# A WKV recurrence and a squared-ReLU feed-forward on one core: another hand-written order of the same instructions

## The chip, the cores and the metric

The kernel runs on one core of one Trainium2 chip. The metric is the device time of one execution in microseconds (us), the median of the runs. A core has a matrix engine (TensorE, PE in the profile; its weight loads are listed as PEld), three engines for elementwise work (VectorE is DVE, ScalarE is ACT, GpSimd is POOL), and SyncE (SP), which here only issues DMAs.

## The reference

The first stage is a recurrence over 768 steps for 4 batches and 8 heads of width 48, with a decay `w` for each step and channel; the second is a feed-forward layer on the 3072 rows that it gives:

```python
for t in range(S):                     # r, k, v, w: (4, 8, 768, 48), u: (8, 48)
    cur = np.einsum('bhd,bhe->bhde', u[None] * kt, vt)
    y[:, :, t] = np.einsum('bhd,bhde->bhe', rt, state + cur)
    state = wt[:, :, :, None] * state + np.einsum('bhd,bhe->bhde', kt, vt)
...
x = attn_out.transpose(0, 2, 1, 3).reshape(B * S, H * D)      # (3072, 384)
h = x @ w_in                                                  # w_in: (384, 2048)
g = np.maximum(h, 0.0) ** 2
return g @ w_out                                              # w_out: (2048, 384), output float32
```

## The kernel before

The 3072 rows are cut into 12 steps of 256 rows, three for each batch (steps 0 to 2 are batch 0). Within a step, two rows share a partition (index `j`), and the 128 partitions are two chunks of 64 (index `c`). The state is carried from chunk to chunk and from step to step of a batch.

What runs on which engine and in which order is written out by hand: `ORDER` is one long string of words, and the program calls one small function for each word from left to right. On each engine the instructions run in the order in which their words stand; between engines only semaphores order them. A word is `name.step...`; `=A`, `=V` or `=G` names the engine (ACT, DVE, POOL), and `:0` to `:3` or `:n`, `:m` a PSUM bank. There are two wide accumulators `att` (banks 0 and 1 for `cum_`, `su_`, `y_` and `p_`) and four narrow ones `one` (banks 0 to 3 for `m1_`, `m2_`, `pw_`, `tr_`, `yt_`; `p_ ... :n` uses 0 and 1 of them).

One step s runs through these words (line of the profile in brackets):

- `ld.s.w`, `.r`, `.k`, `.v`: loads of 384 KB each, issued by SP (L212). `ld.g.i` and `ld.g.o` load quarter g of the input and output weights, 768 KB each (L220, L225); `cast.i.g` and `cast.o.g` round them to 16 bits (L232). `ld.0.u` is a row that `ub_` and `uc_` spread over the partitions.
- `ww_` (L297) multiplies the two rows' decays, `lw_` (L301) takes the logarithm, `cum_` (L341 to L345) sums it over the rows by matmuls, `exp_` and `ac_` (L358, L363) take exponents. `ni_` (L353) replaces one of the matmuls in steps 8 to 11.
- `rw_` and `kw_` (L309, L313) multiply r and k by a decay, `rd_.s.0` and `rd_.s.1` (L376) multiply r and k by the summed decays. Step 0 does this in halves, `rd_.0.i.f`.
- `tr_` (L385) transposes the two on PE in steps 0 to 2, and `rkt_` (L390) copies them out of PSUM; from step 3 on `dtr_` (L393) transposes them by DMA.
- `p_` (L410) multiplies the transposed pair, `pm_` (L418, L421) masks the product. `su_` (L433) forms the new part of the state, `ts_` (L441, L443) adds the old one, `sn_` (L447) applies the decay. `v_` (L305) rounds v.
- `ku_`, `qp_`, `q_`, `vq_` (L316, L321, L324, L327) form the term of the step's own row with u.
- `y_`, `yq_`, `yc_`, `yb_`, `yd_` (L460) add up the stage's output, `ysb_` (L510, L512) copies it out; `yt_` and `xt_` (L520, L525) transpose it on PE in steps 0 to 3, `dyt_` (L528) by DMA from step 4 on.
- `m1_.s.0` to `.7` (L538): the first product of the feed-forward, six matmuls each; `rl_` (L545 on ACT, L547 on DVE) the ReLU, `sq_` (L553, L555) the square. Words 0 and 1 need weight quarter 0, words 2 and 3 quarter 1, and so on.
- The second product: `m2_.s.c.q` (L561, four matmuls, output quarter q) and `os_` (L567, L569) in steps 0 to 4. Steps 5 to 11 use a scheme with seven half-size products, `pw_.s.1` to `.7` (L615), with sums of blocks formed by `tw_` (L580) and `sw_` (L593), and `cx_` and `ow_` (L620 to L634) for the results. `store` (L639) writes them.
- `warm_.n.i` (L643) is n matmuls on zeros whose result nobody reads.

Of the kernel before, what the change touches and what calls it, by code (L numbers as in the profile page):

```python
# [27 lines left out]
rw_.2=G rl_.0.6=A ld.3.o ku_.2=G rl_.1.0=A m1_.1.2:3 m1_.1.4:1 sq_.0.0=A rd_.2.0 tr_.2.1:0 m1_.1.6:2 rl_.1.2=V
rl_.1.4=A m1_.1.1:1 rl_.1.6=V qp_.2=G m1_.1.7:3 rkt_.2.1=V tr_.2.0:2 rl_.1.7=V v_.2=G m1_.1.3:0 rkt_.2.0=V cast.o.0=A
m1_.1.5:3 ac_.2 cast.o.1=G ld.3.k sq_.0.2=A sq_.0.1=A rl_.1.1=V m2_.0.1.0:2 rl_.1.3=A q_.2 sq_.1.0=A p_.2.1:0 su_.2:1  # L30
vq_.2=G sq_.1.1=A m2_.0.1.1 m2_.0.0.0:0 m2_.1.0.0:1 ts_.2.0=V ld.3.r sn_.2.0=G pm_.2.1 m2_.1.0.1 ww_.3=G yc_.2:1
sq_.0.3=A rl_.1.5=A cast.o.2=A yq_.2 p_.2.0:0 sq_.1.2=V m2_.0.0.1 m2_.1.1.0:3 pm_.2.0 lw_.3 sq_.1.3=A m2_.0.0.2
ww_.4=G cum_.3:0 ld.3.v ld.4.r ld.4.k exp_.3 kw_.3=G cast.o.3=A yb_.2 y_.2 m2_.1.1.1 ku_.3=V m2_.1.1.2 m2_.0.1.2
rd_.3.1 rw_.3=G ysb_.2=A lw_.4 m2_.0.1.3 m2_.1.1.3 dtr_.3.1 qp_.3=G rd_.3.0 cum_.4:1 ac_.3 exp_.4 os_.0.1=A os_.1.1=V
m2_.1.0.2 yt_.2:3 tw_.3=V m2_.0.0.3 xt_.2=A rw_.4=G q_.3 m2_.1.0.3 dtr_.3.0 os_.0.0=A kw_.4=G ku_.4=G m1_.2.2:3 ac_.4
os_.1.0=A rd_.4.0 m1_.2.0:0 rl_.2.2=A m1_.2.3:2 ld.4.v v_.3=A rd_.4.1 m1_.2.1:3 rl_.2.0=A su_.3:1 ld.5.w rl_.2.3=A
ld.5.k ld.5.r vq_.3=V p_.3.0:0 rl_.2.1=A ld.7.w m1_.2.6:1 m1_.2.4:2 ts_.3.0=V pm_.3.0 sq_.2.0=A sn_.3.0=G m1_.2.7:3
v_.4=G rl_.2.6=A ts_.3.1=V tw_.1=V yc_.3:1 yq_.3 sq_.2.1=A rl_.2.4=A rl_.2.7=A p_.3.1:0 m2_.2.1.0:0 m1_.2.5:1 ld.5.v
pm_.3.1 rl_.2.5=V ww_.5=G lw_.5 sq_.2.3=A qp_.4=V q_.4 sn_.3.1=G rw_.5=G kw_.5=G y_.3 store.0.1 yb_.3 su_.4:0 dtr_.4.0
m2_.2.0.0:2 ts_.4.0=V ww_.7=G ysb_.3=A m2_.2.0.1 sq_.2.2=A yt_.3:3 cum_.5:1 m2_.2.1.1 m2_.2.0.2 m2_.2.1.2 exp_.5  # L40
sn_.4.0=V store.1.1 rd_.5.1 dtr_.4.1 xt_.3=A m2_.2.1.3 ts_.4.1=V rd_.5.0 v_.5=G vq_.4=G ld.6.w os_.2.1=A m1_.3.4:1
m1_.3.2:3 m1_.3.0:0 ld.6.k rl_.3.4=A ac_.5 rl_.3.2=A rl_.3.0=A dtr_.5.1 sn_.4.1=V ku_.5=V qp_.5=V tw_.2=V m2_.2.0.3
su_.5:1 p_.4.1:0 m1_.3.5:3 ts_.5.0=V os_.2.0=A rl_.3.5=A m1_.3.1:0 pm_.4.1 m1_.3.3:2 dtr_.5.0 rl_.3.1=A m1_.3.7:3
sq_.3.0=A kw_.6=G rl_.3.3=V yc_.4:1 yq_.4 p_.4.0:0 m2_.3.1.0:1 pm_.4.0 sq_.3.2=A sq_.3.1=A rl_.3.7=A m1_.3.6:2 ld.6.r
ld.7.k ld.8.k ww_.6=G sn_.5.0=G ku_.6=G y_.4 yb_.4 ysb_.4=A q_.5 p_.5.0:0 pm_.5.0 store.2.1 m2_.3.1.1 m2_.3.0.0:0
vq_.5=G lw_.6 dyt_.4 tw_.4=V cum_.6:1 p_.5.1:0 rw_.6=G pm_.5.1 rl_.3.6=A exp_.6 m2_.3.0.1 m2_.3.0.2 m2_.3.1.2 ld.7.r
rd_.6.1 ku_.7=G lw_.7 sq_.3.3=A ld.6.v yc_.5:0 yq_.5 y_.5 m2_.3.1.3 dtr_.6.1 os_.3.1=A qp_.6=V rd_.6.0 kw_.7=G
m1_.4.3:2 m2_.3.0.3 rw_.7=G ac_.6 m1_.4.1:1 rl_.4.3=V yb_.5 rl_.4.1=A store.2.0 ysb_.5=V cum_.7:1 q_.6 v_.6=G qp_.7=G
m1_.4.2:3 dtr_.6.0 ac_.7 exp_.7 dyt_.5 m1_.4.0:2 rl_.4.2=A m1_.4.7:1 rl_.4.0=A m1_.4.5:3 vq_.6=G rd_.7.1 os_.3.0=A
rd_.7.0 m1_.4.6:2 rl_.4.7=A ld.7.v m1_.4.4:1 q_.7 sq_.4.0=V rl_.4.5=A rl_.4.6=A ld.8.r ld.8.w su_.6:0 p_.6.0:1  # L50
ts_.6.0=V sq_.4.3=A rl_.4.4=A m1_.5.6:0 pm_.6.0 sn_.6.0=G m1_.5.4:3 ts_.6.1=V m1_.5.7:2 rl_.5.7=A rl_.5.4=A v_.7=G
ku_.8=V p_.6.1:1 yq_.6:0 yc_.6 m1_.5.0:1 m1_.5.5:2 pm_.6.1 rl_.5.6=V rl_.5.0=A m2_.4.0.0:3 sq_.4.2=A sq_.4.1=A
m1_.5.2:1 qp_.8=G sn_.6.1=G rl_.5.5=A y_.6 ww_.8=G su_.7:1 yb_.6 q_.8 dtr_.7.1 dtr_.7.0 ld.9.w m2_.4.0.1 m2_.4.1.0:0
m2_.4.0.2 ts_.7.0=V rw_.8=V rl_.5.2=A vq_.7=V sn_.7.0=V ld.8.v store.1.0 ysb_.6=A lw_.8 sq_.5.3=A cum_.8:0 dyt_.6
ts_.7.1=V kw_.8=V ac_.8 sq_.5.2=A m2_.4.1.1 p_.7.0:1 m2_.4.0.3 ni_.8=V sn_.7.1=G exp_.8 m1_.5.1:2 m1_.5.3:1 m2_.4.1.2
sw_.5.1.1=G store.0.0 pm_.7.0 ld.9.k rl_.5.3=A ld.10.w ld.9.r ww_.9=G vq_.8=G rd_.8.1 m2_.4.1.3 sw_.5.1.2=V rl_.5.1=A
os_.4.0=A rd_.8.0 m1_.6.6:1 os_.4.1=V sq_.5.0=V yc_.7:1 yq_.7 p_.7.1:0 kw_.9=G dtr_.8.0 pm_.7.1 m1_.6.5:2 m1_.6.7:3
m1_.6.4:0 v_.8=A rl_.6.6=A y_.7 lw_.9 sq_.5.1=A sw_.5.0.1=V rl_.6.5=A sw_.5.0.2=V ku_.9=V sw_.5.0.3=V su_.8:0
ts_.8.0=V rl_.6.4=A store.3.0 yb_.7 ysb_.7=A m1_.6.1:2 rl_.6.1=A dtr_.8.1 m1_.6.3:1 sn_.8.0=G rw_.9=V pw_.5.1:0 dyt_.7
sq_.6.2=A rl_.6.3=V cum_.9:1 cx_.5.1=V pw_.5.2:2 ni_.9=V ww_.10=V rl_.6.7=A m1_.6.0:1 ld.9.v exp_.9 ld.10.k ow_.5.1=V  # L60
m1_.6.2:3 sq_.6.3=A rl_.6.0=V rd_.9.1 pw_.5.5 sw_.5.0.4=G sw_.5.1.4=G p_.8.0:0 ac_.9 cx_.5.3=A pm_.8.0 pw_.5.6
m1_.7.2:1 qp_.9=G rd_.9.0 pw_.5.3 rl_.6.2=A rl_.7.2=A sq_.6.0=A yc_.8:0 yq_.8 ld.11.w dtr_.9.1 p_.8.1:1 ku_.10=G
# [638 lines left out]
```

## Time and profile before

| | us |
|---|---|
| median of 3 runs | 177.27 (177.14 to 177.4) |
| the profiled execution, its own time | 178.94 |
| its span, first to last instruction | 177.2 |
| PE busy | 167.7 |
| PE weight loads busy | 132.9 |
| DVE busy | 148.6 |
| ACT busy | 128.6 |
| POOL busy | 113.1 |

The times of single instructions below are from the profiled execution, from the start of its span. Matmuls are pipelined, so a row's duration for one matmul is longer than the distance to the next; the distances between starts tell what PE needs. The granted clock of PE is 1.0 throughout.

### The profile page before, as it was taken

The page shows a single profiled execution, that of the slowest core. Times are in us where ns is not written, and L with a number is a line of the kernel's source. Part 1 is how long each engine was busy: PE and PEld are TensorE (multiplying, and loading weights), DVE is VectorE, ACT ScalarE, POOL GpSimd, SP SyncE. Part 2 cuts the span into 40 slices and gives each one's busy share as a digit, 9 for nine tenths or more (in the row PEclk, how much of TensorE's full clock was granted, in tenths as well). Part 3 has the DMA queues.
Part 4 walks back from the last instruction along what each step waited for, and adds up shares of the span by engine and source line. Part 5 has one row for each costly group of instructions (what it writes and reads, how often), then busy time and mean ns, then how long its engine had stood idle before and what let it go on. Part 6 is the DMA issues. An engine that isn't in the chain of part 4 may idle for free.

```text
span 177.2 us, 6475 instructions
## 1 busy us (share of the span) xinstructions
PE 167.7 (95%) x2772; PEld 132.9 (75%) x2774; DVE 148.6 (84%) x235; ACT 128.6 (73%) x213; POOL 113.1 (64%) x108
## 2 busy tenths in 40 slices
...
GB/s 151 315 311 350 367 266 357 230 369 286 218 257 233 237 256 191 304 253 101 286 199 306 233 156 286 172 238 236 134 257 67 51 45 41 140 89 4 89 10 167
DMA packets 82669, 36.58 MB, mean 206 GB/s; under 512 B 75857, under 2 KB 81106, under 8 KB 82642
## 3 DMA queue, kind: packets, MB, share of 16 engines
...
## 4 chain that ended last, share of the span: by engine, by line
PE 76%; DMA 13%; POOL 4%; DVE 2%; SPq 1%; issue 1%; ACT 0%; DVEq 0%
PE one L538 29%; PE one L615 18%; PE one L561 15%; PE att L460 6%; DMA rkT_b<-rdec_buf 6%; DMA w_st_b<-in_moe_w_out_dram 5%; PE att L410 3%; DMA u_row<-in_u_dram 2%; PE att L433 2%; SPq L212 1%; POOL ku_b L316 1%; PE att L343 1%; POOL wo_sb L232 1%; DVE pmT_b L418 1%; POOL k_b L313 1%
## 5 line engine op out<-in xcount | busy, mean ns | idle before, releaser
L538 PE MATMUL one<-xT_b,wi_sb 128*128 128x256 bf16 x576 | 70.9, 273 | 0.5 <-DVE xT_b L525 0.5
L538 PEld LDWEIGHTS <-wi_sb 128*128 128x128 f16 x576 | 54.7, 98 | 9.1 <-issue 1.2
L545 ACT ACTIVATE gt_b<-one 128x512 f16<-128x512 f32 x73 | 42.1, 598 | 16.2 <-PE one L538 14.8
L553 ACT ACTIVATE gt_b<-gt_b 128x1024 bf16<-128x1024 f16 x39 | 40.1, 1052 | 0.1
L561 PE MATMUL one<-wo_sb,gt_b 128*128 128x384 f16 x160 | 29.5, 326 | 0.4 <-POOL wo_sb L232 0.4
L421 DVE TENSOR_TENSOR pmT_b<-att,mask 128x1024 bf16<-128x1024 f32 x22 | 26.8, 1218 | 1.9 <-PE att L410 1.8
L615 PEld LDWEIGHTS <-gt_b 128*128 128x128 bf16 x280 | 23.5, 98 | 0.6 <-issue 0.2
L561 PEld LDWEIGHTS <-gt_b 128*128 128x128 bf16 x160 | 14.8, 98 | 9.5 <-issue 0.6
L547 DVE TENSOR_SCALAR gt_b<-one 128x512 f16<-128x512 f32 x23 | 15.5, 684 | 3.2 <-ACT gt_b L545 1.9
L447 POOL TENSOR_TENSOR S_b<-t_b,ac_buf 128x192 bf16<-128x192 f32 x16 | 8.8, 551 | 13.8 <-DVE t_b L443 7.7
L327 POOL TENSOR_TENSOR vq_b<-v_b,q_b 128x768 bf16<-128x768 f32 x10 | 15.5, 1550 | 2.7 <-DVE q_b L324 2.7
L615 PE MATMUL one<-wo_sb,gt_b 128*128 128x192 f16 x168 | 16.5, 246 | 0.0
L316 POOL TENSOR_TENSOR ku_b<-k_b,u_bc 128x768 f32<-128x768 f32 x8 | 14.5, 1815 | 2.9 <-ACT u_bc L249 1.8
L313 POOL TENSOR_TENSOR k_b<-k_b,w_b 128x384 f32<-128x384 f32 x10 | 11.0, 1099 | 7.1 <-DMA k_b<-in_k_dram 7.1
L321 POOL TENSOR_TENSOR ku_b<-ku_b,r_b 128x768 f32<-128x768 f32 x8 | 14.9, 1858 | 0.5 <-DVE pmT_b L421 0.4
L309 POOL TENSOR_TENSOR r_b<-r_b,w_b 128x384 f32<-128x384 f32 x9 | 10.7, 1185 | 5.0 <-DMA r_b<-in_r_dram 4.8
L324 DVE TENSOR_REDUCE q_b<-ku_b 128x16 f32<-128x768 f32 x12 | 11.4, 946 | 1.7 <-POOL ku_b L321 1.7
L376 DVE TENSOR_TENSOR rdec_buf<-k_b,att 128x768 bf16<-128x768 f32 (+1 forms) x13 | 11.4, 885 | 1.0 <-POOL k_b L313 0.9
L376 DVE TENSOR_TENSOR rdec_buf<-r_b,att 128x768 bf16<-128x768 f32 (+1 forms) x13 | 11.5, 885 | 0.3 <-POOL r_b L309 0.3
L358 ACT ACTIVATE att<-att 128x768 f32<-128x768 f32 x12 | 9.6, 797 | 2.7 <-PE att L345 2.3
L615 PE MATMUL one<-w_st_b,gt_b 128*128 128x192 f16 x112 | 11.4, 246 | 0.0
L593 POOL TENSOR_TENSOR w_st_b<-w_st_b,gt_b 128x512 bf16<-128x512 bf16 x4 | 5.0, 1250 | 7.5 <-DVE w_st_b L593 7.5
...
## 6 DMA issues: line engine op xcount, KB each, us to landing
...
rkT_b<-rdec_buf SPq DMA_TRANSPOSE x18, 4.4
```

What stands on the lines that cost most here:

```text
L313: product("kw_", s)(k_raw[:, :, 0, :], k_raw[:, :, 1, :], w_raw[:, :, 1, :])
L316: product("ku_", s)(buf("ku", s)[:], buf("k", s)[:, :, 1:3, :], u_bc[:, :, None, :].to_broadcast([C, H, 2, D]))
L321: product("qp_", s)(ku[:], ku[:], buf("r", s)[:, :, 0:2, :])
L327: product("vq_", s)(buf("vq", s)[:].rearrange("p j h d -> p h j d"), buf("v", s)[:], buf("q", s)[:, :, :, None].to_broadcast([C, H, 2, D]))
L376: nc.vector.tensor_mul(rdec[:, i, :, heads, 0:D], x.rearrange("p h j d -> p j h d"), decay[:, None, :, :].to_broadcast([C, 2, n, D]))
L421: nc.vector.tensor_mul(pmT, ps_p[:].rearrange("p e (a x) -> p (e a) x", a=2), mk.to_broadcast([C, 4, 2 * C]))
L538: nc.tensor.matmul(ps1[:, j, :], wi_sb[:, n // 4, kk, n % 4 * 128:(n % 4 + 1) * 128], xT[:, :, kk, :], start=(kk == 0), stop=(kk == KT - 1))
L545: nc.scalar.activation(rl, m1, AF.Relu, scale=RS)
L547: nc.vector.tensor_scalar(out=rl, in0=m1, scalar1=RS, scalar2=0.0, op0=ALU.mult, op1=ALU.max)
L553: nc.scalar.activation(gt, rl, AF.Square)
L561: nc.tensor.matmul(m2, gt[:, n, c * C:(c + 1) * C], wo_sb[:, n, :], start=(n == 0), stop=(n == NT - 1))
L615: nc.tensor.matmul(where_to, gt[:, n, :], wo[:, n, :], start=(n == 0 and i in (1, 2, 5)), stop=(n == NT // 2 - 1), skip_group_check=True)
```

## The change

Only the string `ORDER` is replaced. Both strings have 934 words, and apart from `warm_` the same ones. They differ in the place of the words, in the engine of some (`=`), and in banks (`:`). The idle matmuls of the opening are cut otherwise: 2, 9, 1, 1, 1, 9 before and 1, 3, 6, 5, 3, 12 after. Net changes of engines: seven `rl_` from ACT to DVE, four `rkt_`, three `ysb_` and three `ts_` from DVE to ACT, two `sq_` from DVE to ACT, three `os_` from ACT to DVE, four weight casts off ACT (three to POOL, one to DVE), three `ku_` from POOL to DVE and three `qp_` from DVE to POOL. The opening up to the first `m1_`, and the places of step 2 and step 10 that the text speaks of:

```diff
-ld.0.w ld.0.r warm_.2.3 ld.0.k ld.0.u ww_.0=V lw_.0 ld.0.v warm_.9.0 rw_.0=G ld.1.w ld.1.r cum_.0:1 kw_.0=V exp_.0
-ub_:0 ld.1.k rd_.0.0.1 warm_.1.2 warm_.1.2 rd_.0.1.1 uc_=A ku_.0=G tr_.0.0.1:1 ld.1.v rd_.0.1.0 rkt_.0.0.1=A
-tr_.0.1.1:3 warm_.1.2 rkt_.0.1.1=A tr_.0.1.0:0 ww_.1=G rd_.0.0.0 ld.0.i v_.0=A rkt_.0.1.0=V tr_.0.0.0:2 ld.2.i
-p_.0.1:0 ac_.0 rkt_.0.0.0=V su_.0:1 qp_.0=G pm_.0.1 ld.1.i lw_.1 ts_.0.0=A p_.0.0:n ld.3.i ld.2.w cum_.1:0 kw_.1=G
-pm_.0.0 warm_.9.3 ac_.1 exp_.1 q_.0 ld.2.k rw_.1=G v_.1=A rd_.1.1 sn_.0.0=G vq_.0=G rd_.1.0 tr_.1.1:3 yc_.0:0 yd_.0
-cast.i.0=A ld.2.r rkt_.1.1=V tr_.1.0:2 y_.0 rkt_.1.0=V yq_.0 ts_.0.1=V p_.1.1:n ku_.1=G ysb_.0.1=A p_.1.0:1 sn_.0.1=G
-pm_.1.1 ysb_.0.0=A yt_.0.1:2 cast.i.2=A su_.1:0 yt_.0.0:3 xt_.0.1=V xt_.0.0=V qp_.1=V m1_.0.0:2 ts_.1.0=V cast.i.1=A
...
+ld.0.w ld.0.r ld.0.k warm_.1.1 warm_.3.3 ld.0.u warm_.6.1 ld.1.w ww_.0=V ld.0.v lw_.0 cum_.0:1 warm_.5.0 exp_.0
+kw_.0=V rw_.0=V ld.1.v ub_:0 rd_.0.0.1 uc_=A rd_.0.0.0 ld.1.r tr_.0.0.1:3 ld.1.k ww_.1=G rkt_.0.0.1=A rd_.0.1.1
+tr_.0.0.0:0 rd_.0.1.0 rkt_.0.0.0=A tr_.0.1.1:2 ld.0.i v_.0=G rkt_.0.1.1=A warm_.3.1 ld.2.i ld.2.w ku_.0=V tr_.0.1.0:1
+p_.0.1:0 rkt_.0.1.0=A ac_.0 pm_.0.1 qp_.0=G p_.0.0:n lw_.1 su_.0:1 ld.1.i ts_.0.0=A pm_.0.0 ld.3.i cum_.1:0 warm_.12.2
+q_.0 ld.2.r kw_.1=G ac_.1 exp_.1 rw_.1=G rd_.1.1 sn_.0.0=G v_.1=A cast.i.0=A rd_.1.0 vq_.0=G tr_.1.1:3 yd_.0:0 ku_.1=G
+ld.2.k tr_.1.0:0 rkt_.1.0=V ts_.0.1=V qp_.1=G rkt_.1.1=A yq_.0 yc_.0 y_.0 sn_.0.1=V p_.1.1:n ysb_.0.1=A su_.1:1
+ysb_.0.0=A yt_.0.1:2 pm_.1.1 xt_.0.1=A yt_.0.0:3 p_.1.0:0 xt_.0.0=A cast.i.2=A ts_.1.0=V m1_.0.0:3 ww_.2=G ld.2.v
+pm_.1.0 sn_.1.0=V m1_.0.1:0 m1_.0.5:2 cast.i.1=G q_.1 rl_.0.5=A m1_.0.4:1 rl_.0.4=A lw_.2 vq_.1=V ts_.1.1=V rl_.0.1=A
+y_.1:0 m1_.0.3:2 yc_.1 yq_.1 rl_.0.0=V cast.i.3=G yd_.1 ld.0.o ysb_.1=A ld.1.o cum_.2:1 m1_.0.2:1 exp_.2 rw_.2=G
...
+rkt_.2.0=A q_.2 ld.3.r m1_.1.0:0 rl_.1.4=A m1_.1.5:2 ld.3.o p_.2.1:0 ww_.3=V rl_.0.6=V p_.2.0:1 m2_.0.0.0:1 cast.o.1=G
+rl_.1.0=A sq_.1.0=A lw_.3 rl_.1.5=A sq_.1.1=A sq_.1.3=A ld.4.w vq_.2=G sn_.2.0=G m2_.0.0.1 pm_.2.1 m2_.0.1.0:0
...
+cx_.6.2=A pw_.6.5 v_.10=A cx_.6.3=A pw_.6.7 exp_.11 rl_.8.7=A m1_.8.6:3 rd_.10.0 qp_.10=G rw_.11=G ow_.6.4=V rd_.10.1
+pw_.6.3 rl_.8.6=A kw_.11=V pw_.6.4 dtr_.10.0 m1_.8.0:2 pw_.7.1:3 v_.11=A dtr_.10.1 store.5.1 q_.10 ow_.6.2=V ac_.11
+ow_.6.3=A vq_.10=G rd_.11.0 ac_.10 rl_.8.0=A rd_.11.1 sq_.8.3=A cx_.7.1=V m1_.9.1:1 m1_.9.4:0 rl_.9.1=A pw_.7.2:2
+ow_.7.1=V sw_.7.1.2=G p_.10.0:0 su_.10:1 dtr_.11.0 dtr_.11.1 m1_.9.6:1 ts_.10.0=V pm_.10.0 sn_.10.0=G pw_.7.5 pw_.7.6
...
```

130 lines of the change are left out of this document (61 added, 69 removed).

## The prediction

> **What bounds the kernel now.** I read the page's busy times first, then stretches of the span, then the waits, and then the opening in order of time, since the change is an order and only shows where an engine stands idle. The page and three stretches (columns: us; busy us and count of PE, PE weight loads, DVE, ACT, POOL; clock, DMA share, GB/s):
>
> ```profile
> span 177.2 us, 6475 instructions
> ...
> PE 167.7 (95%) x2772; PEld 132.9 (75%) x2774; DVE 148.6 (84%) x235; ACT 128.6 (73%) x213; POOL 113.1 (64%) x108
> ```
> ```profile
> 10.00:15.00 5.00, 3.38 (x66) 1.82 (x67) 4.62 (x7) 2.86 (x7) 5.00 (x6) 1.00 1.05 325
> 15.00:20.00 5.00, 3.98 (x147) 3.02 (x144) 4.11 (x9) 3.50 (x4) 3.84 (x4) 1.00 1.01 355
> ...
> 120.00:130.00 10.00, 10.00 (x124) 9.22 (x119) 9.31 (x19) 8.85 (x16) 5.22 (x4) 1.00 0.80 190
> ```
>
> TensorE (PE) is full from about 20 us on at the full granted clock; its holes lie before that, where the DMA engines are full (share 1.01 to 1.05). The waits of PE say how little is left after the opening (us in total, times, longest):
>
> ```profile
> PE one L538 <- DVE xT_b L525: 0.5, 1, 0.5
> ...
> PE one L561 <- POOL wo_sb L232: 0.4, 1, 0.4
> PE att L410 <- DMA rkT_b<-rdec_buf: 0.4, 1, 0.4
> PE one L615 <- DVE w_st_b L634: 0.4, 1, 0.4
> ```
>
> The list changes no product except idle `warm_` matmuls: the same matmuls stand in both orders. So the time is the sum of PE's own stream, which stays, the empty time before the first `m1_` (here at 20.00), the few waits after it, and the tail. The opening in order of time (start, duration, what; in brackets the idle time before it and what ended it):
>
> ```profile
> 12.74 1.00 POOL L313 TENSOR_TENSOR k_b<-k_b,w_b 128x384 f32<-128x384 f32 x1
> ...
> 13.69 1.00 POOL L309 TENSOR_TENSOR r_b<-r_b,w_b 128x384 f32<-128x384 f32 x1
> ...
> 14.73 0.95 DVE L376 TENSOR_TENSOR rdec_buf<-r_b,att 128x768 bf16<-128x768 f32 x1
> ...
> 15.12 1.48 POOL L327 TENSOR_TENSOR vq_b<-v_b,q_b 128x768 bf16<-128x768 f32 x1
> 15.60 0.68 DVE L390 COPY rkT_b<-one 128x1024 bf16<-128x1024 bf16 x1
> ...
> 15.83 0.51 PE L460 MATMUL att<-S_b,rkT_b 64*64 64x48 bf16 x24 [0.43 <-DVE rdec_buf L376]
> ...
> 16.50 1.47 ACT L232 CAST wi_sb<-w_st_b 128x1536 f16<-128x1536 f32 x1 [2.37 <-DMA w_st_b<-in_moe_w_in_dram]
> ...
> 17.68 0.42 PE L410 MATMUL one<-rkT_b 64*64 64x128 bf16 x16
> ...
> 17.88 0.85 ACT L512 CAST y_sb_b<-att 128x384 bf16<-128x384 f32 x2
> ...
> 18.13 1.29 DVE L418 TENSOR_TENSOR pmT_b<-one,mask 128x512 bf16<-128x512 f32 x2 [0.24 <-PE one L410]
> ...
> 19.33 0.61 DVE L525 COPY xT_b<-one 128x384 bf16<-128x384 bf16 x2
> ...
> 20.00 3.61 PE L538 MATMUL one<-xT_b,wi_sb 128*128 128x256 bf16 x30 [0.50 <-DVE xT_b L525]
> ...
> 20.77 1.47 ACT L232 CAST wi_sb<-w_st_b 128x1536 f16<-128x1536 f32 x1 [0.66 <-DMA w_st_b<-in_moe_w_in_dram]
> ```
>
> To be seen: `kw_.1` (12.74), `rw_.1` (13.69), `rd_.1.0` (14.73) and then PE at 15.83 form one chain; the first cast of the input weights waits for its landing at 16.5; the copies `rkt_.1.*` are on DVE and run beside that cast; the last link is `xt_.0.*` on DVE, behind `pm_.1.1`.
>
> **The opening, step by step.** Two things that the title names stand in both lists: `ld.0.r` is second and `ld.0.i` is ahead of every load of step 2. What moves on SP's queue is `ld.1.w` ahead of `ld.0.v`, `ld.1.v` ahead of `ld.1.r` and `ld.1.k`, and `ld.2.w` ahead of `ld.1.i` and `ld.3.i`. All loads pass through one queue of full DMA engines, so a load that changes places takes the landing of the place. The two tiles' issues and landings over the first 20 us:
>
> ```profile
> L212 SPq DMA_DIRECT2D k_b<-in_k_dram x3: 1059/1529/5577, 1.9 to 13.7; - x3
> ...
> DMA to landing us min/median/max: 4.8/5.2/11.6
> ```
> ```profile
> L212 SPq DMA_DIRECT2D v_b<-in_v_dram x2: 389/769/1149, 4.2 to 8.2; - x2
> ...
> DMA to landing us min/median/max: 4.1/4.6/5.1
> ```
>
> The second load of v was issued at 8.2 and took 5.1: 13.3. That place is now k of step 1's. So `kw_.1` on POOL starts at 13.4 and not at 12.74, `rw_.1` ends at 15.4, and `rd_.1.0` runs 15.4 to 16.35 where it ended at 15.68: 0.67 later. POOL is emptier before that (`rw_.0` and `ku_.0` go to DVE, `v_.0` comes), but it now waits for the landing, so this gives nothing. On DVE `rw_.0` and `ku_.0` come ahead of `pm_.0.1`, `pm_.0.0` and `q_.0`; these end by about 14.3, still ahead of the 14.4 at which `kw_.1` lets `rd_.1.1` go, so they cost nothing; if k of step 1 landed earlier they would be late next, by up to the 0.6. PE waits with `yd_.0` for `rd_.1.0`, as it did with `yc_.0`, to 16.5.
>
> The larger step is on ACT: `rkt_.1.1` moves from DVE to ACT and behind `cast.i.0` in its order. That cast waits for the same bytes as before, so it runs 16.5 to 17.97 again, though `tr_.1.1` is done by 16.1. What the copy costs on ACT follows from two copies of other sizes:
>
> ```profile
> L525 ACT COPY xT_b<-one 128x768 bf16<-128x768 bf16 x2 | 1.6, 806 | 0.0
> ...
> L390 ACT COPY rkT_b<-one 128x512 bf16<-128x512 bf16 x2 | 1.1, 588 | 0.3 <-PE one L385 0.3
> ```
>
> 512 elements take 588 ns, 768 take 806, so 1024 take 1.02 us: `rkt_.1.1` ends at 19.0, and `p_.1.1` starts at 19.05 instead of 17.68. Behind it on ACT are the two `ysb_.0` (0.85: to 19.85) and the two `xt_.0` (estimated like them, 0.85: to 20.75). `xt_.0` no longer waits for `pm_.1.1`, which gives part of the delay back. `m1_.0.0` starts at 20.8: **0.8 later**. From below: if ACT is free of the cast by then, what is late next is `vq_.0` (1.48 after `sn_.0.0` behind `rw_.1`, to 17.35), then `yq_.0`, `yc_.0`, `y_.0`, the copies and transposes, and `m1_.0.0` at 20.3, 0.3 later. I take 0.8, because the 16.50 is a landing and nothing ahead of it in the queue gets shorter.
>
> The quarters `i.1` and `i.3` land one load later, 384 KB at 325 GB/s, 1.2 us: 22.0 for the first (20.77 above). It is cast on POOL to 23.5; PE arrives at `m1_.0.3` after four `m1_` and `y_.1`, at 24.0. Nothing, then; without that cover up to 0.5. The warm matmuls stand where PE is idle anyway (12 before `tr_.1.1`, done at about 15.2, and it starts at 15.45).
>
> **A rule against the change.** Products that move to DVE beside a busy POOL may not run beside it. The trace has such a pair (the third row is the mean of DVE's four `ku_`):
>
> ```profile
> 42.00 1.00 POOL L313 TENSOR_TENSOR k_b<-k_b,w_b 128x384 f32<-128x384 f32 x1 [2.40 <-DMA k_b<-in_k_dram]
> 42.03 1.79 DVE L316 TENSOR_TENSOR ku_b<-k_b,u_bc 128x768 f32<-128x768 f32 x1 [1.97 <-DMA k_b<-in_k_dram]
> ```
> ```profile
> L316 DVE TENSOR_TENSOR ku_b<-k_b,u_bc 128x768 f32<-128x768 f32 x4 | 4.6, 1159 | 2.0 <-DMA k_b<-in_k_dram 2.0
> ```
>
> The other three took (4.6 - 1.79)/3 = 0.95, so this one lost about 0.84. The Trainium skill, page "SBUF — State Buffer", section "SBUF: two separate sides", says that a DVE instruction with two SBUF inputs and a GpSimd instruction share a port pair under an exclusive lock, and that the later one blocks fully. By that rule, and the trace agrees here with 1.79 against 0.95, `ku_.0` would wait for `v_.0` and the sum would be 177.8 and not 177.7. From the rows alone: `ku_.0` takes between 0.95 and 1.79, the landing of k covers most of it, and 0 to 0.1 reaches `rd_.1.1`; I take 0.
>
> **After the opening.** The second quarter of the output weights is cast at 33.87, which PE awaited:
>
> ```profile
> 33.87 1.47 POOL L232 CAST wo_sb<-w_st_b 128x1536 f16<-128x1536 f32 x1 [1.23 <-DMA w_st_b<-in_moe_w_out_dram]
> ...
> 35.38 2.76 PE L561 MATMUL one<-wo_sb,gt_b 128*128 128x384 f16 x16 [0.42 <-POOL wo_sb L232]
> ...
> 38.39 0.39 PE L410 MATMUL att<-rkT_b 64*64 64x128 bf16 x16
> ```
>
> `ld.1.o` has the same bytes ahead of it in both lists, so the cast ends at 35.35 again. PE would come 0.8 later and finds it done: the wait of 0.42 goes. `p_.2.0` (0.39) moves ahead of that matmul, so the wait stays gone with a smaller delay too. Net here: 0.8 - 0.42 = **0.4 later**.
>
> In the middle, two waits of 0.4 remain in the list above. For the matrix transposes by DMA (rows of 120 to 140 us, and two pieces of the chain that price PE's words):
>
> ```profile
> DMA to landing us min/median/max: 3.0/4.2/4.4
> ```
> ```profile
> 126.82 1.31 PE one L538 x12
> 128.13 3.30 PE one L615 x40
> ```
>
> One `m1_` or `pw_` is 0.655. Step 9's last transpose gets 5.3 us of PE work ahead of its user where it had 3.7, so its 0.4 goes. Step 10's last `rd_` has seven such words, 4.6 us, ahead of `p_.10.0`, where it had 8.7; it needs 0.95 + 3.0 to 4.4: a wait of 0 to 0.8. The other 0.4 (before a `pw_`, on DVE) may go or come. Over the whole, ACT gives away, net, 7 `rl_` (598 ns, the row below), four weight casts (1.47) and three `os_`, and takes four `rkt_`, three `ysb_` and two `sq_`: about -3 us. POOL takes three of the casts and three `qp_` for three `ku_`: about +3. DVE comes out at about +1.5. They are idle for 29 to 64 us of the span, so none becomes the bound over the whole.
>
> ```profile
> L545 ACT ACTIVATE gt_b<-one 128x512 f16<-128x512 f32 x73 | 42.1, 598 | 16.2 <-PE one L538 14.8
> ```
>
> I put the middle at 0, between -0.8 and +1.2. The tail has the same last `pw_`, `ow_.11.3` and one store in both lists: 0.
>
> The sum, made on the profiled run (178.94 us with its span of 177.2, that is 1.7 above the median of the three runs, so I carry differences): 0.8 - 0.42 + 0, **0.4 later; 177.27 + 0.4 = 177.7 us**.
>
> **Rivals.** *Faster:* the opening is set by landings, not by ACT. If the first weight quarter is cast before `tr_.1.1` is done, `m1_.0.0` slips by 0.3 only, the wait of 0.42 at 35.38 hides it, and the waits at step 9's transposes and before the `pw_` go: 0.3 - 0.42 - 0.8, 176.4 us. It decides from a landing before about 15.5; the 16.50 speaks against it, the lighter POOL for it. *Same:* the slip is 0.8 but one of the two middle waits goes and nothing comes: 177.3. *Much slower:* the short distance of step 10 and the DMA transposes of steps 4 and 5, which also get less PE work behind them, each make PE wait 0.5: 0.4 + 1.3, 179.0. For it: the waits of the middle are on just such transfers; against it: the queue ahead of them is shorter. *No change of what the title names:* true for the two loads as said, it has no price of its own.
>
> **Chances.** A run of this kernel can be told from another by about 0.2%, 0.35 us. The forecast (0.3 to 0.9 later) 0.40, much slower 0.17, same 0.18, faster 0.25. The edge of the forecast's case lies within 0.35 for a small part, so: faster 0.25, within 0.2% 0.20, slower 0.55. The range runs from 176.4, the faster case whole, to 179.2, the much slower case and 0.2 for a first cast later than 16.5; what lies outside, waits on several transposes at once or none at all, I give 0.2.
>
> **What would show it.** In the changed profile: `kw_.1` on POOL idle until k's landing at about 13.3; an ACT copy of 128x1024 into `rkT_b` at about 18.0, right behind the cast at 16.5, about 1.0 long; the first `m1_` at 20.3 to 20.8; no wait of PE on `wo_sb` at 35; PE full after it with waits of about 1 us in sum. A first `m1_` at 20.0 or earlier, or a PE wait of over 1 us on a transpose, would make it wrong.

## The result, and the profile after

The changed kernel took **179.66 us** (median of four runs, 178.87 to 181.06) against 177.34 for the kernel before (four runs, 177.14 to 177.46): a ratio of 1.0128, 95% interval 1.0089 to 1.0167, **1.3% slower**, 2.3 us. The forecast was 177.7 us, 0.4 us slower. A second set (e9 below) gave 1.0137 (1.0091 to 1.0184). Some executions of most kernels were in a slower state of the chip and are left out of the ratios; the profiles of e11, e14 and e17 caught one, so no size is read from them.

Below, "after" is the changed kernel, and e1 to e18 are the experiments. A number such as 1.0137 (1.0091 to 1.0184) is the ratio to runs of the kernel before on the same chip, with its 95% interval.

The page of the profiled execution (its own time 180.04 us):

```profile
span 178.3 us, 6502 instructions
PE 169.9 (95%) x2781; PEld 133.4 (75%) x2781; DVE 145.9 (82%) x234; ACT 127.1 (71%) x212; POOL 115.8 (65%) x110
q8 instruction: 22, 0.36, 0.8%
```

The opening in order of time (start, duration, engine, what; in brackets the idle time before it and what ended it), from the timeline:

```profile
9.62 0.82 POOL L305 CAST v_bf_b<-v_b 128x768 bf16<-128x768 f32 x1 [0.19 <-DMA v_b<-in_v_dram]
...
9.71 1.54 DVE L316 TENSOR_TENSOR ku_b<-k_b,u_bc 128x768 f32<-128x768 f32 x1
...
14.01 1.00 POOL L313 TENSOR_TENSOR k_b<-k_b,w_b 128x384 f32<-128x384 f32 x1 [0.86 <-DMA k_b<-in_k_dram]
...
16.14 1.47 ACT L232 CAST wi_sb<-w_st_b 128x1536 f16<-128x1536 f32 x1 [1.33 <-DMA w_st_b<-in_moe_w_in_dram]
...
17.52 1.00 ACT L390 COPY rkT_b<-one 128x1024 bf16<-128x1024 bf16 x1
...
18.97 0.86 ACT L512 CAST y_sb_b<-att 128x384 bf16<-128x384 f32 x2 [0.45 <-ACT rkT_b L390]
...
19.89 0.86 ACT L525 COPY xT_b<-one 128x384 bf16<-128x384 bf16 x2
...
20.80 0.38 PE L538 MATMUL one<-xT_b,wi_sb 128*128 128x256 bf16 x2 [0.22 <-ACT xT_b L525]
```

This is the chain of the prediction, link by link: `kw_.1` (14.01) waits for k, `rkt_.1.1` (17.52) stands behind the cast, and the first `m1_` starts at 20.80. The waits of PE behind the opening (us in total, times, longest), first after, then in a profile of the kernel before with eight idle matmuls at its very end instead of one (e2 below). The first line of e2's list is the wait ahead of the first `m1_` itself:

```profile
PE one L538 <- DMA xT_b<-y_sb_b: 0.5, 1, 0.5
PE one L538 <- ACT xT_b L525: 0.2, 1, 0.2
PE att L410 <- DMA rkT_b<-rdec_buf: 0.2, 1, 0.2
```
```profile
PE one L538 <- DVE xT_b L525: 0.6, 1, 0.6
PE one L615 <- DVE w_st_b L634: 0.4, 1, 0.4
```

To be seen: after, a matrix transpose by DMA (`dyt_`, into `xT_b`) holds PE. In e2, which has the order of before, none does, and there is no wait on `wo_sb` or on `rkT_b` either: the 0.42 and the 0.4 that the prediction read were of the one execution shown. Last, the tail: SP's issue of `store.11.0`, the last store but one, after and before.

```profile
173.30 1.59 SPq L639 DMA_DIRECT2D out_dram<-w_st_b  x1
```
```profile
173.54 0.33 SPq L639 DMA_DIRECT2D out_dram<-w_st_b  x1
```

The DMA view of after for 172 to 175 us shows what moved at that time: the stores on q1, and one packet on q8.

```profile
q1 hardware_dynamic: 276, 0.28, 27.6%
q8 instruction: 1, 0.02, 3.3%
```

It is the 22nd fetch of program code on that queue, 16 KB, 172.96 to 174.52; before there were 21, the last at 162.91. The two stores issued just ahead of the slow one were late too: they landed 3.6 and 3.5 us behind their issue, where the same two took 1.6 and 1.9 in a second profile of after (e9). The first explanation to test was therefore this fetch: after has seven more idle matmuls, 14 more instructions on PE, and PE's program, if this queue serves it, passes one 16 KB step more.

A table cuts every profile into three parts: the start of the first `m1_`, the **stretch** from there to the start of the last matmul of the last `pw_`, and the **tail** from there to the end of the span (us, from the traces):

| kernel | first `m1_` | stretch | tail | span |
|---|---|---|---|---|
| before, as shown to the prediction | 20.00 | 153.46 | 3.70 | 177.2 |
| before, 8 idle at the end (e2) | 20.07 | 151.55 | 3.70 | 175.3 |
| before, 4 idle at the end (e3) | 20.79 | 151.85 | 3.70 | 176.3 |
| before, 16 small idle (e5) | 19.94 | 151.77 | 4.06 | 175.8 |
| before, after's opening parts (e8) | 21.15 | 151.58 | 3.69 | 176.4 |
| after | 20.80 | 152.49 | 4.97 | 178.3 |
| after, again (e9) | 19.82 | 155.11 | 3.50 | 178.4 |
| after, 12 small idle (e12) | 19.96 | 153.55 | 5.01 | 178.5 |
| after, opening undone (e7) | 19.90 | 153.05 | 3.46 | 176.4 |
| after, copy on DVE (e10) | 21.50 | 152.78 | 3.39 | 177.7 |
| after, `dyt_.6` first (e16) | 19.97 | 152.25 | 3.68 | 175.9 |

The execution of before on which the sum was made had 1.6 to 1.9 us more in its stretch than the four others of the same order. Against e2 the changed kernel lost 0.73 in the opening, 0.94 in the stretch and 1.27 in the tail, 2.94 in all, which is the difference of the spans. Each row is one execution; 22 runs of the kernel before on one chip lay between 177.13 and 179.49 us, so one row tells how large a part can be, and not how large it is in the median.

### The profile page after: what moved, and what is told of

It is laid out like the page before. It is cut to its first block, busy times and chain, and to the rows that moved or that the text cites. A ratio compares the mean times of both kernels' runs of the same rounds, so it can differ in the third digit from the quotient of the medians.

```text
span 178.3 us, 6502 instructions
## 1 busy us (share of the span) xinstructions
PE 169.9 (95%) x2781; PEld 133.4 (75%) x2781; DVE 145.9 (82%) x234; ACT 127.1 (71%) x212; POOL 115.8 (65%) x110
## 4 chain that ended last, share of the span: by engine, by line
PE 80%; DMA 9%; SPq 4%; ACT 1%; POOL 1%; issue 1%; DVE 1%
PE one L538 33%; PE one L615 17%; PE one L561 15%; PE att L460 7%; SPq L212 4%; DMA k_b<-in_k_dram 3%; PE att L410 3%; DMA xT_b<-y_sb_b 3%; DMA rkT_b<-rdec_buf 3%; PE att L433 2%; PE att L343 1%; PE one L520 1%; PE one L385 1%; ACT gt_b L553 1%; POOL k_b L313 1%
## 5 line engine op out<-in xcount | busy, mean ns | idle before, releaser
L538 PE MATMUL one<-xT_b,wi_sb 128*128 128x256 bf16 x576 | 70.1, 273 | 0.7 <-DMA xT_b<-y_sb_b 0.5
L545 ACT ACTIVATE gt_b<-one 128x512 f16<-128x512 f32 x66 | 38.1, 598 | 13.6 <-PE one L538 12.8
L553 ACT ACTIVATE gt_b<-gt_b 128x1024 bf16<-128x1024 f16 x41 | 42.2, 1053 | 0.1
L561 PE MATMUL one<-wo_sb,gt_b 128*128 128x384 f16 x160 | 29.0, 327 | 0.0
L321 POOL TENSOR_TENSOR ku_b<-ku_b,r_b 128x768 f32<-128x768 f32 x11 | 20.3, 1843 | 4.8 <-DVE ku_b L316 4.7
L547 DVE TENSOR_SCALAR gt_b<-one 128x512 f16<-128x512 f32 x30 | 20.2, 684 | 2.9 <-PE one L538 2.7
L297 POOL TENSOR_TENSOR ww_b<-w_b 128x384 f32<-128x384 f32 x8 | 8.0, 1000 | 9.3 <-DMA w_b<-in_w_dram 9.3
L447 POOL TENSOR_TENSOR S_b<-t_b,ac_buf 128x192 bf16<-128x192 f32 x17 | 9.8, 579 | 5.8 <-DVE t_b L443 3.4
L593 POOL TENSOR_TENSOR gt_b<-gt_b 128x512 bf16<-128x512 bf16 x7 | 8.3, 1187 | 5.3 <-PE att L460 2.7
L510 ACT CAST y_sb_b<-att 128x768 bf16<-128x768 f32 x11 | 8.8, 798 | 3.9 <-PE att L460 3.9
```

Of the source, the lines that this page charges most:

```text
L321: product("qp_", s)(ku[:], ku[:], buf("r", s)[:, :, 0:2, :])
L538: nc.tensor.matmul(ps1[:, j, :], wi_sb[:, n // 4, kk, n % 4 * 128:(n % 4 + 1) * 128], xT[:, :, kk, :], start=(kk == 0), stop=(kk == KT - 1))
L545: nc.scalar.activation(rl, m1, AF.Relu, scale=RS)
L547: nc.vector.tensor_scalar(out=rl, in0=m1, scalar1=RS, scalar2=0.0, op0=ALU.mult, op1=ALU.max)
L553: nc.scalar.activation(gt, rl, AF.Square)
L561: nc.tensor.matmul(m2, gt[:, n, c * C:(c + 1) * C], wo_sb[:, n, :], start=(n == 0), stop=(n == NT - 1))
```

## The experiments

**Idle matmuls: the program fetch, and the clock.** e1 takes seven idle matmuls away from after; e2 and e3 add seven and three at the end of before.

```diff
 # e1, on after
-... ld.3.i cum_.1:0 warm_.12.2
+... ld.3.i cum_.1:0 warm_.5.2
 # e2 and e3, on before
-warm_.1.5 ow_.11.3=V store.11.1.0
+warm_.8.5 ow_.11.3=V store.11.1.0     (e3: warm_.4.5)
```

> The changed kernel with five idle matmuls in its last opening group instead of twelve, so that its PE program has as many instructions as the kernel before (14 fewer: a matmul and a weight load each). Theory A (the 16 KB program fetch on instruction queue q8 at 172.96 us, the 22nd, is the loss: it falls beside the last stores and a store's issue takes 1.59 us instead of 0.33): q8 shows 21 fetches and none after about 163 us, the issue of the fourth-last store takes 0.3 to 0.4 us, the last store lands about 2.2 us after the last ow_ and not 3.3, and the time falls by 1.5 to 2.5 us to 177.0 to 178.0. Rival B (the order itself makes the tail slow, by its stores' places): the tail and the time stay, 179.2 to 180. Rival C (the opening's 0.8 us and stalls in the middle are the loss): the time stays at 179.2 to 180, with m1_.0.0 at 20.8 as before.

> The kernel before with eight idle matmuls in the last warm_ group, where it had one, next to the last ow_: 14 PE instructions more, which brings its program to the length of the changed kernel's. Theory A: a 22nd fetch on q8 appears at about 172 to 173 us, a store's issue near it takes over 1 us, and the time rises by 1.3 to 2.3 us to 178.6 to 179.6 with a wider scatter. Rivals B and C: nothing new in the tail; seven matmuls at the end, which nothing waits for, and the time stays at 177.2 to 177.6.

> The kernel before with four idle matmuls in that group instead of one: 6 PE instructions more. A dose between. Theory A: a fetch comes or does not, as a whole: either 21 fetches and 177.2 to 177.5 us, or 22 and 178.6 to 179.6; nothing between. If idle matmuls cost by their number: 0.4 times what eight cost. Rivals B and C: 177.2 to 177.6.

e1: 1.0151 (1.0102 to 1.0201), no gain. The fetch was gone and the tail was 3.49 instead of 4.97, as theory A said; but the first `m1_` came at 21.93. The windows 13 to 16, 16 to 19 and 19 to 22 us of e1 show why (after their length: busy us and count of PE, PE's weight loads, DVE, ACT, POOL; then PE's granted clock):

```profile
13.00:16.00 3.00, 1.26 (x7) 0.39 (x5) 2.61 (x5) 1.71 (x3) 2.21 (x4) 1.00 1.03 375
16.00:19.00 3.00, 2.57 (x50) 2.00 (x52) 1.57 (x3) 2.39 (x2) 3.00 (x3) 0.71 1.07 350
19.00:22.00 3.00, 2.57 (x103) 2.28 (x102) 2.46 (x7) 1.84 (x5) 2.92 (x3) 0.72 1.05 398
```

PE was busy for 1.26 us of three, and then worked at 0.71 where after had 1.0; from 17.4 to 20.6 us alone the clock was 0.50. The Trainium skill, page "TensorE: Matmul & The Clock Gate", section "What's actually happening", says that the clock falls to half when PE was idle over a window of about 3.4 us; this trace agrees on the half clock, but PE was not idle here, only less busy. In this execution e1 won in the tail and lost in the opening; that the clock is the whole reason for its time is not shown, since one run of e1 kept a mean clock of 1.0 and still took 179.64 us, as much as after. e2: 1.0009 (0.9977 to 1.0041), e3: 1.0027 (0.9992 to 1.0062): nothing that shows. In e2 the 22nd fetch was there, but at 176.88, behind the end of the span, where it harms nothing. Theory A in its simple form falls: more instructions alone cost nothing.

**The fetch moved.** e5 puts 32 cheap PE instructions into an idle hole of before; e12 puts 24 into after; e6 takes 14 away from after at other places than e1.

```diff
 # e5, on before (tiny_.n.i: n idle matmuls of 64 columns)
-pm_.0.0 warm_.9.3 ac_.1
+pm_.0.0 warm_.9.3 tiny_.16.3 ac_.1
 # e12, on after
-cum_.1:0 warm_.12.2
+cum_.1:0 warm_.12.2 tiny_.12.2
 # e6, on after
-ld.0.k warm_.1.1 warm_.3.3 ld.0.u ... rkt_.0.1.1=A warm_.3.1 ld.2.i
+ld.0.k ld.0.u ... rkt_.0.1.1=A ld.2.i
```

> The kernel before with 16 further idle matmuls of 64 columns behind warm_.9.3, where PE stands idle from 13.9 to 14.8 us: 32 more PE instructions, so that the 22nd program fetch is asked for some 18 instructions ahead of PE's end and not behind it. Theory D (two losses: about 1.2 us in the opening by the late landing of k of step 1 and the copy behind the cast, and 1.3 us in the tail by a program fetch among the last stores; the kernel with fewer idle matmuls lost the second but fell to a clock of 0.71 in the opening, 0.9 us): m1_.0.0 at 19.3 as before, the fetch at 171 to 174 us, from the last ow_ to the end of the span 4.0 to 4.6 us instead of 3.0, and the time 1.0 to 1.6 us over before, 178.6 to 179.2. Rival E (the whole loss is the opening; the long tail of the one profile was chance): 177.3 to 177.9, the tail 2.8 to 3.1 with the fetch in it.

> The changed kernel with 12 further idle matmuls of 64 columns behind warm_.12.2, where PE is idle to 16.0 us: 24 more PE instructions, so that the last program fetch is asked for some 38 instructions ahead of PE's end, ahead of the last three stores. Theory F: the fetch at 171 to 172.5 us, the last product 3.7 to 4.2 us ahead of the span's end, the time 0.5 to 1.2 below the changed kernel's of this batch if that one has the long tail. Rival E: the time the same within 0.4, the tail 3.4 to 3.5.

> The changed kernel without its first four idle matmuls and without the group of three at 9.6 us, the twelve at 12.7 us kept: 14 PE instructions fewer, so no 22nd fetch before the end, and PE is still fed before the first products. Theory D: clock 1.0 in 16 to 22 us, m1_ words from 20.5 as in the changed kernel, the tail 2.8 to 3.1 us, time 178.2 to 178.8, 1.0 to 1.5 below the changed kernel. Rival E: the tail was 2.8 to 3.1 in most of its runs anyway, and the time stays at 179.3 to 180.

The issue of the store beside the fetch, in e5 (fetch at 170.23 to 171.18) and in e12 (172.60 to 173.77), by the timeline of SP:

```profile
170.43 1.13 SPq L639 DMA_DIRECT2D out_dram<-w_st_b  x1
```
```profile
172.83 1.31 SPq L639 DMA_DIRECT2D out_dram<-w_st_b  x1
```

So in three profiles of two orders a store issued while the fetch ran took 1.1 to 1.6 us where the last stores otherwise take 0.33 to 0.43. (e13 below is a fourth, 1.02 us.) What it costs hangs on the place: in e5, two stores earlier, the tail was 4.06 instead of 3.70 and the time unchanged, 0.9974 (0.9929 to 1.0019); in e12 it was 5.01, and the time 1.0147 (1.0101 to 1.0192), not below after's 1.0137, so moving the fetch by 24 instructions gained nothing. The Trainium skill, page "Runtime: NRT & Kernel Launch", section "Instruction fetch mechanics", states blocks of 16 KiB or 256 instructions and calls a block's cost "mostly hidden". The size agrees (16 KB, and the last two fetches of after lie 247 rows of PE and its weight loads apart). Beside the last stores the fetch isn't hidden; what the earlier fetches cost was not looked at. e6 came out at 1.0141 (1.0066 to 1.0217): no fetch and a tail of 3.38, but the first `m1_` at 21.60, and again a lower clock in the opening:

```profile
10.00:13.00 3.00, 2.12 (x76) 1.78 (x75) 1.85 (x2) 2.57 (x7) 1.90 (x3) 0.86 1.14 342
13.00:16.00 3.00, 2.80 (x28) 1.32 (x19) 2.97 (x5) 1.96 (x5) 2.83 (x4) 0.57 1.03 382
```

With all of the change's idle matmuls the clock stayed at 1.00 through the opening in both profiles of after. The clock isn't the whole of e6's loss either: of the four runs in its ratio the two with a mean clock of 1.0 were the longer (182.13 and 182.22 us, against 180.14 and 180.53 at 0.99).

**The opening.** e4 (on e1), e11 and e7 put step 1's loads back; e10 and e7 put the copy back on DVE; e8 puts both parts into before; e18 delays before by a large amount.

```diff
 # loads back, on after (e4 on e1; e7, e11)
-rw_.0=V ld.1.v ub_:0 ... ld.1.r tr_.0.0.1:3 ld.1.k ww_.1=G
+rw_.0=V ld.1.r ub_:0 ... ld.1.k tr_.0.0.1:3 ld.1.v ww_.1=G
 # copy back, on after (e7, e10)
-rkt_.1.0=V ts_.0.1=V qp_.1=G rkt_.1.1=A
+rkt_.1.1=V rkt_.1.0=V ts_.0.1=V qp_.1=G
 # e8, on before: ld.1.w ld.1.v ... ld.1.r ... ld.1.k, and rkt_.1.1=A
 # e18, on before: ld.1.w ld.1.v ... ld.1.r ... ld.0.i ld.1.k
```

> The kernel with five idle matmuls, and SP's loads of step 1 back in the order w, r, k, v where the change has w, v, r, k. By the prediction's chain k of step 1 then lands about 0.6 us earlier, kw_.1 starts at 13.2 to 13.4, and m1_.0.0 comes 0.3 to 0.6 earlier than 20.8, unless the cast of the first weight quarter at 16.1 stays ahead of the copy of rkt_.1.1: then 20.6 to 20.8. Theory A with a neutral opening: the time equals that of the kernel with five idle matmuls alone within 0.4 us, since the wait on the output weights at 35 us takes up to 0.4 of the gain back. Rival C: 0.5 to 0.8 us less than without this edit.

> The changed kernel with step 1's loads in the order w, r, k, v again, the copy left on ACT behind the cast, all twelve idle matmuls kept: the other part. If the copy carries the loss: m1_.0.0 follows the landing of the first weight quarter by 4.3 to 4.7 us, 20.3 to 21.0 with a landing at 15.9 to 16.5, and 0 to 0.4 less time. If the late k carries it: m1_.0.0 at 19.9 to 20.1 and 0.7 to 1.2 less.

> The changed kernel with rkt_.1.1 on DVE ahead of rkt_.1.0 and the late k kept: one of the two parts of the opening. If the copy behind the cast carries the opening's loss (as the prediction had it): m1_.0.0 at 20.0 to 20.2 and 0.6 to 0.8 us less time than the changed kernel. If the late landing of k carries it: m1_.0.0 at 20.5 to 20.8, and 0 to 0.3 less.

> The changed kernel, all idle matmuls kept, with two parts of the opening undone: step 1's loads again in the order w, r, k, v, and rkt_.1.1 on DVE ahead of rkt_.1.0 and not on ACT behind the first weight cast. Theory D: kw_.1 starts at 12.8 to 13.1, the m1_ words at 19.3 to 19.7 instead of 20.5, and the time falls by 0.8 to 1.2 to 178.4 to 178.8, the tail still 4 us and more. Rival E: falls by the same or more, to 178 or below, and the tail is short. If the loss were in the middle: no change, 179.3 to 180.

> The kernel before with those two parts put in and nothing else: loads w, v, r, k of step 1 and rkt_.1.1 on ACT in its place behind the first weight cast. Theory D: kw_.1 at 13.4 to 14.0, the m1_ words at 20.3 to 20.7 instead of 19.3, the time 0.9 to 1.4 over before (178.2 to 178.8), the tail as before. Rival E: 1.5 to 2.3 over before. The prediction's own sum: 0.4 over before, since the wait on the output weights at 35 us would take 0.42 back.

> The kernel before with v of step 1 ahead of r and k of step 1 behind the first quarter of the input weights on SP's queue, two places later than in the change. k lands at about 16.3 instead of 11.5 to 11.9, kw_.1 starts at 16.4 instead of 12.8, and the first m1_ comes 3.2 to 3.7 us later, at about 23.5. If a delay of the opening comes out in full: 3.0 to 3.7 us over before, 180.5 to 181.3. Rival H: 1.5 to 2.5 over before.

e4: 1.0098 (1.0060 to 1.0136), e11: 1.0065 (1.0029 to 1.0102), e10: 1.0052 (1.0016 to 1.0087), **e7: 1.0024 (0.9978 to 1.0071)**. By time, each part undone gives about half of the loss back and both give nearly all, 1.1%. The profiles don't show it in the opening: the first `m1_` of e7 was at 19.90, that of e10 at 21.50 and not at 20.0 to 20.2, with the first weight quarter landing at 18.29 (16.11 in after). e18: 1.0246 (1.0190 to 1.0302); its first `m1_` at 24.36, 4.3 later than e2's (the clock fell as well, to 0.50 at 19 to 22 us), came out as 4.4 us, so a large delay of the opening passes to the end in full. But e8: 0.9976 (0.9935 to 1.0017). The two parts put into before cost at most 0.3 us, though its profile has the first `m1_` 1.1 later than e2's. The expectation of 0.9 to 1.4 was wrong. A part of this is that the openings move by themselves: in four profiles of before's opening (before, e2, e3, e5) the first `m1_` was at 19.94 to 20.79, latest where the first weight quarter landed latest (17.32 in e3, 14.95 to 16.48 in the others).

**After once more.** e9 is the changed kernel itself.

> The changed kernel itself once more, unchanged, beside the three below on one chip. Theory F (the loss has three parts: the opening, 0.8 to 1.2 us; the middle, about 0.9 more waiting on transfers than the kernel before; the tail, 1.5 where a program fetch falls between the last two stores, else 0.2 less than before): 1.5 to 2.5 us over before, m1_.0.0 at 20.6 to 21.0; if the fetch is tied to the place in PE's program it stands again at 172 to 174 us, with a store issue of over 1 us and the last product 4.5 to 5 us ahead of the span's end; if it was chance, 3.4 to 3.5 us. Rival E (all of it the opening): the tail 3.4 to 3.5 and the time still 2.0 to 2.5 over before.

1.0137 (1.0091 to 1.0184), with another profile: the opening no later than before, the fetch at 180.68 and the tail short, and yet the same span. Both signs of being wrong that the prediction had named are in it: a first `m1_` ahead of 20.0, and a wait of over 1 us on a transpose. Its opening, and PE in step 6:

```profile
12.95 0.99 POOL L313 TENSOR_TENSOR k_b<-k_b,w_b 128x384 f32<-128x384 f32 x1
...
15.30 1.47 ACT L232 CAST wi_sb<-w_st_b 128x1536 f16<-128x1536 f32 x1 [0.65 <-DMA w_st_b<-in_moe_w_in_dram]
16.68 1.00 ACT L390 COPY rkT_b<-one 128x1024 bf16<-128x1024 bf16 x1
```
```profile
19.82 0.92 PE L538 MATMUL one<-xT_b,wi_sb 128*128 128x256 bf16 x7 [0.22 <-ACT xT_b L525]
```
```profile
95.81 0.49 PE L561 MATMUL one<-wo_sb,gt_b 128*128 128x384 f16 x2
98.52 0.72 PE L538 MATMUL one<-xT_b,wi_sb 128*128 128x256 bf16 x5 [2.23 <-DMA xT_b<-y_sb_b]
```

PE stood for 2.23 us for `dyt_.6`. SP's queue ahead of that transpose, after and e2 (start, length of the issue, what):

```profile
89.72 1.02 SPq L212 DMA_DIRECT2D r_b<-in_r_dram  x1
90.84 0.77 SPq L212 DMA_DIRECT2D v_b<-in_v_dram  x1
91.66 0.88 SPq L639 DMA_DIRECT2D out_dram<-w_st_b  x1
92.64 1.30 SPq L528 DMA_TRANSPOSE xT_b<-y_sb_b  x1
```
```profile
86.88 0.53 SPq L212 DMA_DIRECT2D w_b<-in_w_dram  x1
87.50 1.15 SPq L212 DMA_DIRECT2D v_b<-in_v_dram  x1
88.70 1.13 SPq L639 DMA_DIRECT2D out_dram<-w_st_b  x1
90.40 1.22 SPq L528 DMA_TRANSPOSE xT_b<-y_sb_b  x1
```

Three transfers stand ahead of it in both. But in e2 SP is done with them and issues the transpose as soon as `ysb_.6` is (90.38); after, `ysb_.6` ended at 91.27 and SP had 1.3 us of issues left. It lands at 93.6 in e2, 1.9 ahead of its user, the weight load of step 6's first `m1_` at 95.50; after at 96.65, and the user starts at 96.79; in e9 at 98.47 and 98.52. The same slack, from the landing to the first weight load that needs it, in the other profiles (us; after's order: after, e7, e9, e10, e12; before's: before, e2, e3, e5, e8):

| slack behind the transpose | before's order | after's order | e13, e16 (words moved, below) |
|---|---|---|---|
| step 6 | 1.01 to 2.15 | 0.04 to 0.14 | 1.37, 2.44 |
| step 8 | 0.19 to 0.96 | 0.04 | 0.34, 0.37 |

So in after's order the landing sets when PE starts step 8 in all five profiles, and step 6 in four of them, in e10 with its first `m1_` at 21.50 as in e9 at 19.82; in after itself it came 0.14 us ahead. The long wait of e9 is mostly a slow transfer: PE got there 0.7 us earlier than in after, and the transpose landed 1.8 us later. At step 8 SP was free: after's `dyt_.8` went out at 114.52, right behind its input (114.50), and then took 4.9 us to land.

**The transposes.** e13 moves four words behind `dyt_.6` and `dyt_.8` on SP's queue, e14 also has the opening of e7; e15 is the reverse in before; e16 and e17 are e13 and e14 with `ld.11.w` left where it was.

```diff
 # e13, e14, on after
-ysb_.6=A ld.8.v sn_.6.1=G ... ts_.7.0=V store.1.0 ku_.8=V ... dyt_.6 m2_.4.0.1
+ysb_.6=A sn_.6.1=G ... ts_.7.0=V ku_.8=V ... dyt_.6 ld.8.v store.1.0 m2_.4.0.1
-ld.11.r ld.11.w v_.9=A ... dyt_.8 rl_.7.4=V
+v_.9=A ... dyt_.8 ld.11.r ld.11.w rl_.7.4=V     (e16, e17: only ld.11.r moves)
 # e15, on before
-dyt_.6 ... store.0.0 pm_.7.0 ld.9.k rl_.5.3=A ld.10.w ld.9.r
+store.0.0 pm_.7.0 ld.9.k rl_.5.3=A ld.10.w dyt_.6 ld.9.r
```

> The changed kernel with four words moved on SP's queue and nothing else: ld.8.v and store.1.0 behind dyt_.6, ld.11.r and ld.11.w behind dyt_.8. Theory G (the transposes of steps 6 and 8 set PE's pace in the middle): dyt_.6 is issued at about 91.4 instead of 92.6 and lands at 94 to 95.5 instead of 96.6, no wait of PE for it; PE's stretch from the first m1_ to the last product 151.8 to 152.3 us instead of 152.5 to 155; time 0.6 to 1.2 below the changed kernel, 178.5 to 179.2. Rival C (the opening alone): the stretch may shorten, the time stays within 0.3 of 179.7 to 179.9.

> The same with the two parts of the opening undone too. Theory G: m1_.0.0 at 19.7 to 20.0, the stretch 151.8 to 152.3, PE's end to the span's end 3.4 to 3.5: a span of 175.1 to 175.8, time 176.9 to 177.6, as fast as the kernel before or up to 0.3 faster. Rival C: no better than with the opening undone alone, 178.5.

> The kernel before with dyt_.6 moved on SP's queue behind store.0.0, ld.9.k and ld.10.w. Theory G: it is issued at about 92.4 to 93.5 instead of 90.4, lands at 96.5 to 97.5, and m1_.6.6, which started at 95.5, waits 1 to 2 us; the time 0.8 to 1.6 over before. Rival C: a wait of PE shows but is taken back later, 0 to 0.3 over before.

> The changed kernel with ld.8.v and store.1.0 behind dyt_.6 and ld.11.r behind dyt_.8 on SP's queue; ld.11.w stays ahead. Theory G: dyt_.6 lands at 94 to 95.5, PE does not wait for it, lw_.11 on ACT is not held (119 to 119.7), PE's stretch from the first m1_ to the last product 152.0 to 152.6 us, time 178.6 to 179.2, 0.6 to 1.2 below the changed kernel. Rival C (the opening alone): 179.5 to 180.

> The same with the opening's two parts undone. Theory G with the opening: m1_.0.0 at 19.7 to 20.0, the stretch 152.0 to 152.6, time 177.2 to 177.9, 1 us below the kernel with the transposes alone and level with the kernel before. Rival H (the opening's delay is swallowed behind it): the same time as e16 within 0.3.

e15: 1.0209 (1.0141 to 1.0277). `dyt_.6` was issued at 92.02 and landed at 98.46, PE waited:

```profile
98.50 0.72 PE L538 MATMUL one<-xT_b,wi_sb 128*128 128x256 bf16 x5 [2.34 <-DMA xT_b<-y_sb_b]
```

One word moved behind three others on SP's queue costs the kernel before 2.1%, 3.7 us, more than expected and more than the wait itself: the reverse works. e13 went wrong by the edit itself, 1.0296 (1.0253 to 1.0340). `dyt_.6` landed at 94.72 and no product waited over 0.2 us for a transpose, but ACT did:

```profile
122.29 0.52 ACT L301 ACTIVATE lw_buf<-ww_b 128x384 bf16<-128x384 f32 x1 [3.44 <-POOL ww_b L297]
```

`ld.11.w` landed at 121.2 instead of 117.1, `ww_.11` on POOL and `lw_.11` on ACT stood for it, the `rl_` of step 8 stood behind `lw_.11`, and PE waited 2.47 us for one of those. e14 has the same fault; its runs scatter from 179.22 to 184.06 us (before: 177.88), and it is not read. **e16: 1.0032 (0.9990 to 1.0075)**, e17: 1.0011 (0.9973 to 1.0050). With `ld.11.w` left alone, putting `ld.8.v` and `store.1.0` behind `dyt_.6` and `ld.11.r` behind `dyt_.8` gives back 1.0% of the 1.4%. In e16 `dyt_.6` is issued at 90.48 and lands at 93.5, and no wait of PE on a transpose is left. Undoing the opening as well adds 0.2%, less than the intervals can tell. (e7, e16 and e17 ran on other chips than e9, so to set them against 1.0137 takes it that the ratio carries over; e10 to e12 ran on e9's.) None of these kernels beats the one before.

## Why the prediction was wrong

**The opening was right, for one landing.** `kw_.1` was expected at 13.4 and came at 14.01, since k landed at 13.94 and not at 13.3; the cast came at 16.14 and not at 16.50. That 20.8 was met with one link late and one early is in part luck. In e9 and e12 k landed at 12.88 and 12.83, the weights at 15.28 and 14.79, and the first `m1_` was at 19.82 and 19.96; in e13 and e16, with the same opening, at 20.11 and 19.97. Over these five the mean is 20.1, and over five profiles of before's opening (before, e2, e3, e5, e15) it is 20.2. The 0.8 is the dear end of a range of about 0 to 0.8, and by these profiles too large as a term of the median; the sum took its landing rows from one execution and treated them as fixed. `ku_.0` lost 0.59 beside `v_.0` on POOL (1.54 against 0.95), within the bounds given. The Trainium skill's lock, page "SBUF — State Buffer", section "SBUF: two separate sides", would have it wait out `v_.0`, and the rows nearly agree: 10.44, the end of `v_.0`, and 0.81 more. It cost the chain nothing, since `kw_.1` still waited for k until 13.94.

**The credit of 0.42 was the first failed step.** The wait on `wo_sb` did vanish, as forecast. But e2, e3, e5 and e8, of the same order as before at that place, don't have it either (0.09 at most, in e5): the shown execution was 1.7 us above its median, and the wait was part of that. To take a difference on that execution and add it to the median counts a gain that the median, as far as these four show, had already. Nor was 0.35 us the step by which two kernels can be told apart: the intervals here are 0.3 to 0.8% to each side.

**"The middle at 0" was the second, and the largest in the mean.** Between five stretches of after without a moved transpose (152.49, 155.11, 153.55, 153.05, 152.78) and four of before (151.55, 151.85, 151.77, 151.58) lie 1.7 us in the mean, or 1.4 with the shown execution of before (153.46) among the latter. The text did name the mechanism, a transpose by DMA with less work behind it, but looked at steps 4, 5, 9 and 10. In these five profiles no wait of over 0.2 us on a `dyt_` came at 4, 5 or 10 (with idle matmuls cut, in e1, e4 and e6, step 4 waited 0.4 to 0.8); it came at 6 and 8. At step 6 `ld.8.r`, `ld.8.v` and `store.1.0` stood ahead of the `dyt_` on a queue that ran late; at step 8 `ld.11.r` and `ld.11.w` went out just ahead of it, and it took 4.4 to 5.0 us to land (3.7 to 4.5 in five profiles of before's order, 4.1 in e13 and e16). The distance was counted in PE's words; SP's queue was not walked through for every transpose. Of the 1.7, waits on the `dyt_` are 1.0 in the mean (0.43 to 2.76, none in the four of before). e16, without them, still has 152.25, 0.4 to 0.7 above before's; no single wait of it behind the first `m1_` is over 0.2 us, and where the rest goes was not found. The busy times behind "the middle" were forecast as about -3 (ACT), +3 (POOL) and +1.5 (DVE) and came out at -1.5, +2.7 and -2.7; none of the three became the bound, as was said.

**"The tail 0" was the third.** By the order it is, if anything, shorter: 3.39 to 3.50 in e7, e9 and e10, 3.68 in e16, against 3.70. With the fetch at the last stores it is 4.97 and 5.01, and 4.71 in e13. It fell there in one of two profiles of after itself, and in e12 and e13; in e9 and e10, with the same program on PE, it came 2.3 and 1.2 us behind the span's end. Thus the warm matmuls, costed at nothing, can cost 1.5 by lengthening the program, and with seven fewer the first `m1_` came at 21.93 and 21.60 (e1, e6) instead of 19.82 to 20.80. What the tail adds to the median is not shown: e9's span is as long as after's without it. By these profiles the sum would have been, as an estimate, about 0 to 0.8 for the opening, 0 for the credit, 1.4 to 1.7 for the middle and -0.3 to 1.3 for the tail, against 2.3 measured.

**The rival "much slower"**, 179.0 by waits on transposes, had the mechanism and a chance of 0.17; it put its waits on steps 4, 5 and 10 and had no tail, so that its 179.0 came nearer to 179.66 than its steps deserve. (The two loads "that the title names" stand in both orders, as the prediction says, and bear on nothing; the title here names none.)

**Not settled.** Moving the transposes (e16) and undoing the opening (e7) each give back some 1.0 to 1.1%, and both together hardly more. That the delays cover each other (what PE loses at the start it need not wait for at step 6) could explain why they don't add; it is not shown. It does not explain why e7, in whose profile the user of `dyt_.6` still starts 0.04 us behind its landing at 96.54, and whose first `m1_` is no earlier than e9's, gained so much in time; nor is e8 explained. Shown is that the queue ahead of the transposes matters, both ways (e15, e16). What decides whether the fetch falls among the stores was not found.
